# A transformer block on one Trainium2 core: attention units of eight heads with one key tile per step, and part of the transposes moved to DMA

## The chip, the cores and the metric

The kernel runs on one core of one Trainium2 chip. A core has engines that run their own instruction streams and wait for each other through semaphores: PE (TensorE, matrix multiplies; PEld is its loading of weights), ACT (ScalarE, functions of one argument such as exp), DVE (VectorE), POOL (GpSimd) and SP (SyncE, which here only issues DMA transfers). A transfer can be issued from SP's queue or from ACT's. On-chip data lies in SBUF; matmuls write to PSUM, which has eight banks of 128 x 512 f32. The metric is the device time of the whole kernel in microseconds (us). Before the change it is 1144.2, the median of 3 runs (1143.97 to 1144.4).

## The reference

One transformer block with adaptive LayerNorm, in bf16. x has 2048 tokens of D = 1024 features, there are 32 heads of 32, all of which share one key head and one value head, and the feed-forward width is F = 3584.

```python
mod = (silu(c) @ w_mod).reshape(1, 6, 1, 1024)
sa, ca, ga, sb, cb, gb = [mod[:, i] for i in range(6)]
h = layernorm(x) * (1 + ca) + sa
q = (h @ wq).reshape(B, S, 32, 32).transpose(0, 2, 1, 3)
k, v = h @ wk, h @ wv                       # one head each
p = softmax(einsum('bhqd,bkd->bhqk', q, k) * 32 ** -0.5)
a = einsum('bhqk,bkd->bhqd', p, v).transpose(0, 2, 1, 3).reshape(B, S, 1024) @ wo
x = x + ga * a
h = layernorm(x) * (1 + cb) + sb
x = x + gb * ((silu(h @ w1) * (h @ w3)) @ w2)
```

(Abridged: reshapes and types are left out.) The exponentials alone are 32 x 2048 x 2048, and they can only be computed on ACT.

## The kernel before, in words

**Tiling.** Tokens go through in eight blocks of 256 queries (`NB`, `B`). The 1024 features of q are eight groups of 128 partitions (`NC`), each of which holds four heads. There are 16 key tiles of 128 (`NTT`). A *unit* is one query block and one group of four heads, and it has eight *steps* (`NJ`), each of two key tiles. A step (`s_exp`, L822) issues eight score matmuls with 32 rows of contraction, two for each head, 256 columns wide, into two pairs of PSUM banks, and then two exponentials of 128 x 1024 on ACT into a slot of `U`, of which there are `NU` = 10. In all there are 512 steps and 1024 exponentials. The scores use six banks (`S6`, L536) as a ring of three pairs; everything else shares two banks (`PB`, L537).

**After a unit's steps** `av` (L853) multiplies the exponentials with V: 64 matmuls of 256 columns that accumulate in one bank and cannot start before the eighth step's exponentials have begun. DVE sums the exponentials over keys: `pairs` (L842) adds the two key tiles of two steps at a time (2048 elements a row), and a tree whose depth `level` (L850) gives adds the results (1024 elements); matmuls with `ONES` finish the sum over partitions. The norm is a transpose of the denominators, a copy of the values, a reciprocal, a transpose back and a multiplication, all on DVE at 256 columns. The result replaces q in `QT`.

**The start.** Loads are issued in the order of L588 to L599, nearly all from SP's queue: x tiles 0 to 3, the first half of w_mod's scale columns (`wm_dma(1, 0)`), x tiles 4 and 5, the second half, x 6 and 7, two features of wq, x 8 to 11, the two halves of the shift columns (`wm_dma(0, h)`), the other six features of wq, x 12 to 15. Only c, wk and wv come from ACT's queue. `lnt1` (L628) takes statistics of a tile of 128 tokens (DVE, POOL), normalizes it, transposes it by eight PE matmuls with `IDENT` and copies it out of PSUM, on ACT or DVE, into `HT`. `mod_cols` (L661) computes scale and shift, and copies the shift to `SAB`; `scale0` (L677) multiplies wk, wv and two features of wq by the scale; `k_bias` (L691) turns the shift into biases of q and k. `k_proj`, `v_proj` and `q_proj` (L729, L744, L759) make keys, values and queries. DMA loads split features as `(p c)`: partition p holds features 8p to 8p+7, and PE reads the normalized tile with a stride of eight elements to match.

**After a block's attention** `wo` (L916) projects, adds the residual, takes LayerNorm 2, transposes with PE into PSUM and applies scale and shift on DVE. The feed-forward part follows as *slabs* of 256 columns of w1 and w3 (L961: 32 matmuls, a tanh on ACT, two DVE operations) and *quarters* of w2 (L998, L1037: 56 matmuls of 256 columns for each quarter of the output). It is done while the next blocks' attention runs: these matmuls are the filler between score groups. The tail, after the last block's exponentials, has the last block's wo, slabs and quarters. For it w2 is loaded in two halves (`w7_dma`, L991) into the then free `U` and `W2S`.

**What sets the order.** The main program (from L1114) only describes operations and what they read and write (`Graph.op`, L55). A greedy planner (`Placer`, L185) goes through the modelled time, picks for each engine the operation with the smallest due time among those that could start soon (`choose`, L275), gives it a PSUM bank (`commit`, L307) and emits it with the waits that it needs (`emit`, L362). A table, `PLAN` (L115), has a row for every 16 steps: how long PE and the others may be kept waiting for a more urgent operation, how long values and filler may not alternate, and offsets on the due times of kinds of operation. So a change of an operation's price, size or place changes the order of everything around it, on each engine and on SP. In the trace all instructions carry line 22, the helper that plays them, and are told apart by their tiles.

Of the kernel before, what the change touches and what calls it, by code (L numbers as in the profile page):

```python
# [42 lines left out]
class Graph:  # L43
# [63 lines left out]
    def alias(self, new, old):  # L107
# [8 lines left out]
    (0.0, 0.11, 0.2, 0, 2.3, {"ln/dve": 20, "ln/act": 104, "mod/pe": -60}),  # L116
    (0.0, 0.13, 0.2, 0, 0.1,
     {"q/pe": -6, "mc/pe": 16, "pair/dve": 3, "av/dve": -10, "an/dve": -17, "slab/dve": -44, "slab/act": 35,
      "wo/dve": -9, "ln/pe": -56, "ln/dve": -21, "k/dve": 4, "mod/pe": -23}),
    (0.0, 0.15, 0.2, 1, 3.5, {"an/dve": 18}),  # L120
    (0.0, 0.15, 0.05, 1, 3.8,
     {"q/pe": -14, "mc/pe": 7, "av/dve": 44, "an/dve": -17, "slab/dve": -44, "slab/act": 35, "wo/dve": -9,
      "ln/dve": -21, "k/pe": -62, "k/dve": 4, "mod/pe": -23}),
    (0.0, 0.15, 0.2, 0, 1.1, {"wo/pe": 4, "q/pe": 1, "mc/pe": 21, "av/dve": 2, "quarter/dve": 23, "mc/dve": -3}),
    (0.0, 0.12, 0.2, 0, 1.4, {"wo/pe": 4, "q/pe": 1, "mc/pe": 21, "av/dve": 2, "quarter/dve": 23, "mc/dve": -3}),
    (0.0, 0.13, 0.2, 0, 1.2, {"av/dve": 34, "ln/dve": 20, "ln/act": 104, "mod/pe": -60, "mc/dve": 42}),
    (0.0, 0.13, 0.2, 0, 1.2, {"wo/pe": 36, "av/dve": 34, "ln/dve": 20, "ln/act": 104, "mod/pe": -60, "mc/dve": 42}),
    (0.0, 0.12, 0.2, 0, 0.8, {"wo/pe": 2, "av/dve": 34, "ln/dve": 20, "ln/act": 104, "mod/pe": -60, "mc/dve": 42}),
    (0.0, 0.12, 0.2, 0, 1.6,
     {"wo/pe": -33, "q/pe": -7, "pair/dve": 6, "wo/dve": -20, "q/dve": -43, "ln/pe": -40, "ln/dve": -10,  # L130
      "ln/act": 32, "mod/pe": -50}),
    (0.0, 0.11, 0.05, 1, 2.3,
     {"wo/pe": 4, "q/pe": 123, "pair/dve": 2, "av/dve": -22, "an/dve": 26, "slab/dve": -91, "mc/dve": -3}),
    (0.0, 0.11, 0.05, 1, 2.3,
     {"wo/pe": 4, "q/pe": 123, "pair/dve": 2, "av/dve": -22, "an/dve": 26, "slab/dve": -91, "mc/dve": -3}),
    (0.0, 0.11, 0.2, 0, 3.4, {"quarter/pe": 8, "pair/dve": 26, "slab/act": -67, "quarter/dve": -45, "mc/dve": 31}),
    (0.0, 0.11, 0.2, 0, 1.6, {"wo/pe": -55, "slab/pe": 31, "mc/pe": -5, "pair/dve": 21, "slab/dve": 16}),
    (0.0, 0.11, 0.0, 0, 2.8,
     {"quarter/pe": 8, "pair/dve": 26, "av/dve": 5, "slab/dve": -62, "slab/act": -67, "quarter/dve": -45,
      "mc/dve": 31}),  # L140
    (0.0, 0.11, 0.02, 1, 2.2,
     {"av/dve": -3, "quarter/dve": 61, "wo/dve": -13, "q/dve": -13, "ln/dve": 20, "ln/act": 104, "mod/pe": -60,
      "mc/dve": 42}),
    (0.0, 0.11, 0.02, 0, 2.6,
     {"wo/pe": -55, "slab/pe": 31, "mc/pe": -5, "pair/dve": 21, "av/dve": 20, "an/dve": 100, "slab/dve": 16,
      "quarter/dve": 84}),
    (0.0, 0.11, 0.02, 0, 2.6,
     {"wo/pe": -55, "slab/pe": 31, "mc/pe": -5, "pair/dve": 21, "av/dve": 20, "an/dve": 100, "slab/dve": 16,
      "quarter/dve": 84}),
    (0.0, 0.11, 0.02, 0, 2.6,  # L150
     {"wo/pe": -55, "slab/pe": 31, "mc/pe": -5, "pair/dve": 21, "av/dve": 20, "an/dve": 100, "slab/dve": 16,
      "quarter/dve": 84}),
    (0.0, 0.11, 0.1, 0, 2.8, {}),
    (0.0, 0.11, 0.2, 0, 1.7, {"slab/pe": 26, "mc/pe": 39, "pair/dve": -5, "slab/dve": 9, "slab/act": -76}),
    (0.0, 0.11, 0.1, 0, 1.5,
     {"wo/pe": -55, "q/pe": -15, "mc/pe": -5, "pair/dve": 21, "av/dve": 6, "slab/act": 13, "quarter/dve": -30}),
    (0.0, 0.11, 0.1, 1, 1.5,
     {"wo/pe": -55, "q/pe": -15, "mc/pe": -5, "pair/dve": 21, "av/dve": 6, "an/dve": -1, "slab/act": 13,
      "quarter/dve": -30}),
    (0.0, 0.11, 0.1, 1, 1.5,  # L160
     {"wo/pe": -55, "q/pe": -15, "mc/pe": -5, "pair/dve": 21, "av/dve": 6, "an/dve": -1, "slab/act": 13,
      "quarter/dve": -30}),
    (0.0, 0.11, 0.1, 0, 1.6, {"wo/pe": -55, "slab/pe": 31, "mc/pe": -5, "slab/act": 13, "quarter/dve": 84}),
    (0.0, 0.11, 0.05, 0, 1.8,
     {"slab/pe": -67, "quarter/pe": -25, "q/pe": -22, "pair/dve": 26, "av/dve": -15, "an/dve": -52,
      "slab/act": -67, "quarter/dve": -169, "mc/dve": 31}),
    (0.0, 0.11, 0.05, 1, 2.4, {}),
    (0.0, 0.11, 0.05, 1, 2.4, {}),
    (0.0, 0.11, 0.2, 0, 1.0,
     {"wo/pe": -55, "q/pe": -20, "mc/pe": 70, "pair/dve": 19, "slab/act": 13, "quarter/dve": -51}),  # L170
    (0.0, 0.11, 0.2, 0, 1.7,
     {"wo/pe": -28, "quarter/pe": 37, "q/pe": -20, "mc/pe": 70, "pair/dve": 19, "an/dve": -19, "slab/act": 13,
      "quarter/dve": -51}),
    (0.0, 0.11, 0.02, 0, 3.6,
     {"wo/pe": -28, "quarter/pe": 37, "q/pe": -20, "mc/pe": 70, "pair/dve": 19, "an/dve": -30, "slab/act": 13,
      "quarter/dve": -51}),
    (0.0, 0.11, 0.05, 0, 4.2,
     {"av/pe": -127, "wo/pe": -27, "quarter/pe": 39, "pair/dve": -46, "av/dve": -102, "wo/dve": 96, "q/dve": 7}),
    (0.0, 0.11, 0.2, 0, 3.2,
     {"av/pe": -127, "wo/pe": -55, "quarter/pe": 39, "q/pe": 66, "pair/dve": -46, "an/dve": 15, "wo/dve": 11,  # L180
      "q/dve": 7}),
# [3 lines left out]
class Placer:  # L185
# [121 lines left out]
    def commit(self, n, e, k, start):  # L307
# [11 lines left out]
        if e == "sp" or n.dma is not None:  # L319
            self.t[e] = start + dur  # L320
            self.bw = max(self.bw, start + 2.6) + n.nbytes / n.bw
            n.fin = self.bw + 0.5
# [119 lines left out]
def build(nc, x_in, wq_in, wk_in, wv_in, wo_in, w1_in, w3_in, w2_in, c_in, wmod_in, out, S, D, F):  # L442
# [34 lines left out]
    RB = sb("RB", [P, 2, B], F32)  # L477
# [9 lines left out]
    RC = sb("RC", [P, 8], F32)  # L487
# [8 lines left out]
    Uf = U[:].rearrange("p a b c d -> p (a b c d)")  # L496
    HTf = HT[:].rearrange("p a b -> p (a b)")
# [16 lines left out]
    GP = HTf[:, o:o + 1024].rearrange("p (s x) -> p s x", s=2)  # L514
# [10 lines left out]
           W2f[:, 0:NC * 512].rearrange("p (c f) -> p c f", c=NC)]  # L525
# [40 lines left out]

    dma("act", SCC[:, 0, :], c_in.rearrange("o (p c) -> p (o c)", p=P), "C", 2048, writes=["C0"], vt=-2000)
    for i, w in enumerate((wk_in, wv_in)):
        dma("act", WKV[:, i], pc(w), ("WKV", i), 65536, writes=[("WKV", i)], vt=-1999)

    def x_dma(tt0, cnt, vt):
# [5 lines left out]
        dma("sp", dst, x2[tt0 * P:(tt0 + cnt) * P, :].rearrange("(t p) d -> p t d", p=P), ("XL", tt0),  # L577
            cnt * P * D * 2, writes=keys, vt=vt, bw=FAST)

    def wm_dma(fld, h, vt):  # L580
        dma("sp", WM0[:, 4 * h:4 * h + 4, fld * D:(fld + 1) * D], pc(wmod_in)[:, 4 * h:4 * h + 4, fld * D:(fld + 1) * D],
            ("WM0", fld, h), 1 << 20, writes=[("WM0", fld, h)], vt=vt, bw=FAST)
# [15 lines left out]
    wq_dma(2, NC, "WQ1", -1890)  # L598
    x_dma(12, 4, -1889)  # L599
# [28 lines left out]
    def lnt1(tt, vt):  # L628
# [13 lines left out]
        static = tt < 6  # L642
# [3 lines left out]
        def tr(b=tt):  # L646
            return [lambda e, cc=cc: e.transpose(
                BANKH[b][:, cc * P:(cc + 1) * P], XN[slot].rearrange("p (q c) -> p c q", c=NC)[:, cc, :],
# [12 lines left out]
    def mod_cols(fld):  # L661
        G.tag = "mod"
        s = Sess()
        for h in range(2):
            op("pe", lambda b, h=h: [lambda e, c=c, k=k: e.matmul(
                BANK[b][:, 64 * k:64 * k + 64], WM0[:, c, fld * D:(fld + 1) * D].rearrange("p (q k) -> p k q", k=NC)[:, k, :],
                SCC[:, 3, c:c + 1].broadcast_to([P, 64]), start=(c == 0 and k == 0), stop=(c == NC - 1), skip_group_check=True)
                for c in range(4 * h, 4 * h + 4) for k in range(NC)], 0.92, reads=["C3", ("WM0", fld, h)],
# [112 lines left out]
    def mod_chunk(i, vt):  # L781
# [4 lines left out]
        if i == 1:  # L786
            G.alias([("WMB", 1)], [("XS", tt) for tt in range(6, 10)])
# [31 lines left out]
    CYC = [(n, f, j) for n in range(NB) for f in range(NC) for j in range(NJ)]  # L819
    exps = {}  # L820

    def s_exp(c):  # L822
        G.tag = "s"
        n, f, j = CYC[c]
# [3 lines left out]
        def mm():  # L828
            return [lambda e, g=g, kk=kk: e.matmul(
                BANK[2 * r[g // 2] + g % 2][:, kk * B:(kk + 1) * B],  # L830
# [350 lines left out]
```

## Time and profile before

| what | us |
|---|---|
| median of 3 runs | 1144.2 |
| profiled execution | 1143.93 |
| its span | 1142.1 |
| start of the first exponential | 32.6 |
| first scores to last scores | 32.1 to 1043.4 |
| end of the exponentials, start of the tail | 1046.1 |
| ACT busy / PE busy / DVE busy | 1024.2 / 1119.6 / 955.0 |
| the 1024 exponentials on ACT, busy | 964.8 |
| sums of exponentials on DVE, busy (2048 / 1024 wide) | 309.9 / 249.6 |

The granted clock of TensorE is 1.000. A busy time of PE is the modelled duration of pipelined matmuls that overlap, so start-to-start times are the better prices: 16 matmuls of 256 columns begin at 1065.11 and the next group at 1066.86. In groups of instructions the name before the arrow is the tile written, the names behind it are those read: `U<-S` is an exponential, `S<-QT,KT` a score, `PB<-U,V` values, `PB<-W2S,HT` a matmul of w2, `PB<-QT,W` one of a slab. W in a name stands for the weights of w1 and w3 and, in the start, of wq.

### The profile page before, as it was taken

To read this page: it belongs to the slowest core of one execution; us is meant where nothing else is said; L and a number is where in the kernel's file an instruction comes from. 1 tells how busy PE (TensorE), PEld (TensorE's weight loads), DVE (VectorE), ACT (ScalarE), POOL (GpSimd) and SP (SyncE) were. 2 spreads that over 40 slices of the span, in tenths; PEclk is the share of its full clock that TensorE was granted. 3 is DMA by queue.
4 is the path that set the end of the run, shared out by engine and by line. 5 is a ranking of instruction groups with operands and counts; after the bars stand their busy time and mean duration, and the time that the engine had idled before them with its cause. 6 is when DMAs were issued, how large, how long until landed. Compare 5 with 4: busy or idle time off the path is not lost.

```text
span 1142.1 us, 34856 instructions
## 1 busy us (share of the span) xinstructions
PE 1119.6 (98%) x15630; PEld 763.8 (67%) x15664; DVE 955.0 (84%) x1555; ACT 1024.2 (90%) x1163; POOL 36.6 (3%) x83
## 2 busy tenths in 40 slices
PE   8999999999999999999999999999999999999999
PEld 7754446666577656776677657766677666776887
DVE  7899899988988889889878989888888987888442
ACT  6999999999999999999899999999999998996110
POOL 4100000000000000000000000000000000000000
PEclk9999999999999999999999999999999999999999
DMA  9511178666396558765596468765596549667793
GB/s 343 180 52 62 38 220 215 177 186 164 81 271 191 148 130 213 225 195 144 142 264 194 142 160 227 199 194 149 133 255 189 152 116 255 200 187 202 223 291 115
DMA packets 361620, 206.32 MB, mean 181 GB/s; under 512 B 4864, under 2 KB 353280, under 8 KB 361472
## 3 DMA queue, kind: packets, MB, share of 16 engines
q1 hardware_dynamic: 361040, 203.97, 63.3%
q8 instruction: 123, 2.02, 0.7%
q14 instruction: 25, 0.20, 0.1%
q10 hardware_dynamic: 432, 0.13, 0.0%
HBM read 199.89 MB, written 4.19 MB: 179 GB/s over the span
## 4 chain that ended last, share of the span: by engine, by line
ACT 55%; PE 41%; DVE 3%; issue 0%; POOL 0%; POOLq 0%
ACT U L22 50%; PE PB L22 29%; PE S L22 12%; ACT HT L22 4%; DVE PS L22 2%; DVE QT L22 0%; DVE ST L22 0%; DVE RB L22 0%; DVE HT L22 0%; DVE X L22 0%; ACT KT L22 0%; ACT PS L22 0%; ACT XNB L22 0%; DVE XNB L22 0%; DVE RC L22 0%
## 5 line engine op out<-in xcount | busy, mean ns | idle before, releaser
L22 ACT ACTIVATE U<-S 128x1024 bf16<-128x1024 f32 x1024 | 964.8, 1117 | 17.1 <-PE PB L22 14.2
L22 DVE TENSOR_TENSOR PS<-U 128x2048 bf16<-128x2048 bf16 x256 | 309.9, 1214 | 15.6 <-ACT U L22 14.3
L22 DVE TENSOR_TENSOR PS<-PS 128x1024 bf16<-128x1024 bf16 x368 | 249.6, 686 | 4.2
L22 PE MATMUL PB<-QT,W 128*128 128x256 bf16 x1856 | 229.4, 273 | 0.2
L22 PE MATMUL S<-QT,KT 32*128 32x256 bf16 x4096 | 203.3, 273 | 5.4 <-ACT U L22 2.5
L22 PEld LDWEIGHTS PB<-QT,W 128*128 128x128 bf16 x1856 | 170.0, 98 | 47.7 <-issue 28.7
L22 PE MATMUL PB<-W2S,HT 128*128 128x256 bf16 x1512 | 191.4, 273 | 0.1
L22 PEld LDWEIGHTS PB<-W2S,HT 128*128 128x128 bf16 x1512 | 136.7, 98 | 45.2 <-issue 27.7
L22 PEld LDWEIGHTS S<-QT,KT 32*128 32x128 bf16 x4096 | 60.7, 92 | 131.9 <-ACT U L22 118.8
L22 PE MATMUL PB<-U,V 128*32 128x256 bf16 x4032 | 124.7, 273 | 1.3 <-DVE X L22 0.5
L22 PE MATMUL PB<-QT,HT 128*128 128x256 bf16 x960 | 120.0, 273 | 0.3 <-DVE HT L22 0.3
L22 PEld LDWEIGHTS PB<-U,V 128*32 128x32 bf16 x4032 | 100.0, 97 | 21.0 <-issue 7.0
L22 ACT ACTIVATE HT<-PB 128x512 bf16<-128x512 f32 (+1 forms) x110 | 78.6, 715 | 32.2 <-PE PB L22 32.2
L22 PEld LDWEIGHTS PB<-QT,HT 128*128 128x128 bf16 x960 | 88.1, 98 | 24.4 <-issue 14.3
L22 PE MATMUL PB<-HT,W 128*128 128x256 bf16 (+1 forms) x561 | 98.5, 316 | 3.5 <-issue 1.8
L22 DVE SCALAR_TENSOR_TENSOR HT<-HT,PB 128x512 bf16<-128x512 bf16 x102 | 69.3, 679 | 30.7 <-ACT HT L22 30.4
L22 DVE TENSOR_TENSOR HT<-HT,PB 128x512 bf16<-128x512 bf16 x102 | 69.6, 682 | 17.9 <-PE PB L22 17.2
L22 PEld LDWEIGHTS PB<-HT,W 128*128 128x128 bf16 x576 | 50.0, 97 | 38.3 <-issue 15.1
L22 PE MATMUL PB<-WO,QT 128*128 128x512 bf16 x213 | 54.0, 380 | 2.4 <-issue 1.3
L22 DVE STREAM_TRANSPOSE RB<-PB 128x256 f32<-128x256 f32 x63 | 28.2, 448 | 30.8 <-PE PB L22 30.8
L22 POOL TENSOR_SCALAR RS<-MV 128x1 f32<-128x1 f32 x32 | 11.5, 358 | 1018.6 <-DVE MV L22 1017.8
L22 ACT ACTIVATE HT<-S 128x512 bf16<-128x512 f32 (+1 forms) x15 | 11.0, 738 | 33.3 <-PE S L22 33.2
(112 smaller groups left out, 682.3 us busy)
## 6 DMA issues: line engine op xcount, KB each, us to landing
W<-in_B_w_dram SPq DMA_DIRECT2D x150, 512.0 KB, 4.6
W2S<-in_B_w_dram SPq DMA_DIRECT2D x28, 1792.0 KB, 8.4
HT<-in_B_w_dram SPq DMA_DIRECT2D x74, 512.0 KB, 4.6
W2S<-in_w_mod_dram SPq DMA_DIRECT2D x8, 1024.0 KB, 5.3
X<-in_A_x_dram SPq DMA_DIRECT2D x8, 512.0 KB, 6.9
U<-in_w_mod_dram SPq DMA_DIRECT2D x4, 1024.0 KB, 11.3
out_dram<-X SPq DMA_DIRECT2D x7, 512.0 KB, 8.0
U<-in_B_w_dram SPq DMA_DIRECT2D x1, 3584.0 KB, 14.0
```

The source lines that it names most:

```text
L22: return getattr(e, call[0])(*call[1], **call[2])
```

## The change

- A unit is two feature groups (eight heads). A step is one key tile: four score matmuls of 512 columns (256 queries of two feature groups). It still has two exponentials of 128 x 1024. A unit has 16 steps, and the total stays 512.
- The values come in halves of eight key tiles: 32 matmuls of 512 columns each. The first half is copied to an f32 buffer, the second is added to it. The sums over keys are adds of 2048 elements throughout; the norm is done once for two feature groups, at 512 columns.
- LN1's tiles 8 to 15 are transposed by eight DMA transposes from SP's queue instead of PE and an eviction. LN2 of blocks 1 to 6 is transposed by two DMA transposes for each block, and scale and shift are then applied in place from SBUF.
- Features are in natural order, `(c p)`, for wq, wk and wv; PE's transposes and the shift and scale columns are read without a stride. Rows of wk and wv become pieces of 64 bytes.
- The scale and shift columns of w_mod are loaded in parts of six and two chunks instead of four and four. Six features of wq and x tiles 12 to 15 are issued from ACT's queue, after c has landed. Four instead of six of LN1's tiles have a fixed bank. `PLAN` has new values.

```diff
-    def wq_dma(f0, f1, key, vt):
-        dma("sp", WQ[:, :, f0 * P:f1 * P], pc(wq_in)[:, :, f0 * P:f1 * P], key, (f1 - f0) << 18, writes=[key], vt=vt,
-            bw=FAST)
+    WSPL = (0, 6, NC)
...
+    def wq_dma(f0, f1, key, vt, eng="sp", after=()):
+        dma(eng, WQ[:, :, f0 * P:f1 * P], cp(wq_in)[:, :, f0 * P:f1 * P], key, (f1 - f0) << 18, writes=[key], vt=vt,
+            bw=FAST, after=after)
+    AL = list(G.last["C0"])
...
-    wq_dma(2, NC, "WQ1", -1890)
-    x_dma(12, 4, -1889)
+    wq_dma(2, NC, "WQ1", -1890, "act", AL)
+    x_dma(12, 4, -1889, "act", AL)
...
+        if tt >= 8:
+            o = op("sp", lambda: [lambda e: e.dma_start_transpose(HT[:, :, tt * P:(tt + 1) * P], XN[slot])], 0.5,
+                   reads=[("XN", slot)], writes=[("HT", cc, tt) for cc in range(NC)], vt=vt, dma=("HTL", slot), nbytes=1 << 18)
+            o.bw = -262144.0 / 1.0 * 1.0
+            return
-        static = tt < 6
+        static = tt < 4
...
-                for c in range(4 * h, 4 * h + 4) for k in range(NC)], 0.92, reads=["C3", ("WM0", fld, h)],
+                for c in range(WSPL[h], WSPL[h + 1]) for k in range(NC)], 0.23 * (WSPL[h + 1] - WSPL[h]), reads=["C3", ("WM0", fld, h)],
...
-    CYC = [(n, f, j) for n in range(NB) for f in range(NC) for j in range(NJ)]
+    CYC = [(n, f, k) for n in range(NB) for f in range(0, NC, 2) for k in range(NTT)]
...
-                BANK[2 * r[g // 2] + g % 2][:, kk * B:(kk + 1) * B],
-                KT[32 * g:32 * (g + 1), (2 * j + kk) * P:(2 * j + kk + 1) * P], QT[32 * g:32 * (g + 1), n, f, :],
-                start=True, stop=True, tile_position=(32 * g, 0)) for kk in range(2) for g in range(4)]
+                BANK[2 * r[g // 2] + g % 2], KT[32 * g:32 * (g + 1), k * P:(k + 1) * P],
+                QT[32 * g:32 * (g + 1), n, f:f + 2, :].rearrange("p c q -> p (c q)"),
+                start=True, stop=True, tile_position=(32 * g, 0)) for g in range(4)]
...
+    def sums(g):
+        w, c0 = g // 2, g * NJ
+        if level(w) == 2:
...
+        d = g % 3
+        for q in range(0, NJ, 2):
+            upair(3 if q else d, c0 + q)
+            if q:
+                fold(d, 3, c0 + q)
...
+                return [lambda e, h=h: e.matmul(
+                    BANK[b][32 * h:32 * (h + 1), :], V[:, NJ * hf + q, :],
+                    U[:, (g * NJ + q) % NU, h].rearrange("p c q -> p (c q)"),
+                    start=(q == 0), stop=(q == NJ - 1), tile_position=(0, 32 * h),
+                    skip_group_check=True) for h in range(4)]
...
+        if hf == 0:
+            G.tag = "an"
+            op("dve", lambda b: [lambda e: e.tensor_copy(A, BANK[b])], 0.575, reads=[("av", g)], writes=ak, vt=vt, sess=s)
+            return
...
+        op("dve", lambda b: [lambda e: e.tensor_tensor(A, A, BANK[b], ALU.add)], 0.605, reads=[("av", g)] + ak,
+           writes=ak, vt=vt, sess=s)
...
+        if 0 < n < NB - 1:
+            for t in range(2):
+                o = op("sp", lambda t=t: [lambda e: e.dma_start_transpose(h2t(n)[:, :, t * P:(t + 1) * P], XN[t])], 1.2,
+                       reads=[("XN", t)], writes=[("h2r", n, t)] + h2k(n), vt=vt - 100, waw=(t == 0), dma=("HT2", t),
+                       nbytes=1 << 18)
+                o.bw = 200e3
```

More of the change, by code (lines that the diff above doesn't have):

```diff
@@ L129 @@
[L129 to L146, printed above, removed]
@@ L182 @@
+    (0.0, 0.11, 0.2, 0, 4.5,
+     {"wo/pe": -51, "slab/pe": -9, "quarter/pe": 34, "mc/pe": -96, "pair/dve": -47, "av/dve": -16, "an/dve": 4,
+      "wo/dve": -52, "q/dve": 88}),
 ]
@@ L786, in mod_chunk @@
         if i == 1:
-            G.alias([("WMB", 1)], [("XS", tt) for tt in range(6, 10)])
+            G.alias([("WMB", 1)], [("XS", tt) for tt in range(7, 11)])
         dma("sp", WMB[r], pc(wmod_in)[:, :, c0:c0 + 512], ("WMB", r), 1 << 20,
@@ new lines, in uk, with add, upair, fold @@
+    def uk(c):
+        return [("U", c % NU, i) for i in range(2)]
+    def add(dst, a, b, ka, kb, vt, tag):
+        G.tag = tag
+        op("dve", lambda: [lambda e: e.tensor_tensor(PSW[:, dst], a, b, ALU.add)], 1.12, reads=ka + kb,
+           writes=psk(dst), vt=vt, post=0.08)
+    def upair(dst, c):
+        add(dst, UW[:, c % NU], UW[:, (c + 1) % NU], uk(c), uk(c + 1), c + 101.0, "pair")
+    def fold(dst, src, c):
+        add(dst, PSW[:, dst], PSW[:, src], psk(dst), psk(src), c + 102.0, "av")
@@ L867, in av, with avp @@
+    hold = {}
+    def avp(n):
+        if n == 0:
+            return W2f[:, 0:D].bitcast(F32), ["AVP"]
+        return GP.bitcast(F32), [("GP", 0)]
+    def av(g):
+        n, f, hf = g // NC, g % NC // 2 * 2, g % 2
+        w = g // 2
+        s = Sess(False)
+        sl = sums(g)
+        hold[g] = sl
+        G.tag = "av"
         for q in range(NJ):
             def mm(b, q=q):
-                return [lambda e, h=h, kk=kk: e.matmul(
-                    BANK[b][32 * h:32 * (h + 1), 0:B], V[:, 2 * q + kk, :], U[:, (u * NJ + q) % NU, h, kk, :],
-                    start=(q == 0 and kk == 0), stop=(q == NJ - 1 and kk == 1), tile_position=(0, 32 * h),
-                    skip_group_check=True) for kk in range(2) for h in range(4)]
@@ L873, in av @@
-            op("pe", mm, 0.2184, reads=[("V", q // 2), ("U", (u * NJ + q) % NU, 0), ("U", (u * NJ + q) % NU, 1)],
-               writes=[("av", u)], vt=-500 + u, mode="A", sess=s, post=0.145, after=[exps[(u * NJ + LAG, 1)]])
-        sd = Sess(lev > 0)
-        for q in range(NJ) if lev == 0 else ():
-            def mu(b, q=q):
-                return [lambda e, h=h, kk=kk: e.matmul(
-                    BANK[b][32 * h:32 * (h + 1), 0:B], ONES[:, 0:32], U[:, (u * NJ + q) % NU, h, kk, :],
-                    start=(q == 0 and kk == 0), stop=(q == NJ - 1 and kk == 1), tile_position=(0, 32 * h),
-                    skip_group_check=True) for kk in range(2) for h in range(4)]
-            op("pe", mu, 0.2184, reads=["ONES", ("U", (u * NJ + q) % NU, 0), ("U", (u * NJ + q) % NU, 1)],
-               writes=[("dn", u)], vt=-500 + u, mode="A", sess=sd, post=0.175, after=[exps[(u * NJ + LAG, 1)]])
@@ L884, in av @@
-        slots = list(range(0, NP, 1 << (lev - 1))) if lev else []
-        for i0 in range(0, len(slots), 2):
-            def md(b, ks=slots[i0:i0 + 2]):
-                return [lambda e, h=h, k=k: e.matmul(
-                    BANK[b][32 * h:32 * (h + 1), 0:B], ONES[:, 0:32], PS[:, k, h, :], start=(k == 0),
-                    stop=(k == slots[-1]), tile_position=(0, 32 * h), skip_group_check=True)
-                    for k in ks for h in range(4)]
-            op("pe", md, 0.109 * len(slots[i0:i0 + 2]), reads=["ONES"] + [("PS", k) for k in slots[i0:i0 + 2]],
-               writes=[("dn", u)], vt=-500 + u, mode="A", sess=sd, post=0.175)
@@ new lines, in av, with md @@
+        for x in ks:
+            def md(b, x=x):
+                return [lambda e, h=h: e.matmul(
+                    BANK[b][32 * h:32 * (h + 1), :], ONES[:, 0:32], PSW[:, x, h * 512:(h + 1) * 512], start=(x == ks[0]),
+                    stop=(x == ks[-1]), tile_position=(0, 32 * h), skip_group_check=True) for h in range(4)]
+            op("pe", md, 0.216, reads=["ONES"] + psk(x), writes=[("dn", w)], vt=-500 + g, mode="A", sess=sd, post=0.175)
+        G.tag = "an"
+        op("dve", lambda b: [lambda e: e.tensor_tensor(A, A, BANK[b], ALU.add)], 0.605, reads=[("av", g)] + ak,
+           writes=ak, vt=vt, sess=s)
```

235 lines of the change are left out of this document (133 added, 102 removed).

## The prediction

> **What bounds the kernel now.** I read the page's totals first, then the stretches around the exponentials, then the chain of waits inside the attention, then the start. Totals and the three groups that the change touches most:
>
> ```profile
> PE 1119.6 (98%) x15630; PEld 763.8 (67%) x15664; DVE 955.0 (84%) x1555; ACT 1024.2 (90%) x1163; POOL 36.6 (3%) x83
> ...
> ACT 55%; PE 41%; DVE 3%; issue 0%; POOL 0%; POOLq 0%
> ...
> L22 ACT ACTIVATE U<-S 128x1024 bf16<-128x1024 f32 x1024 | 964.8, 1117 | 17.1 <-PE PB L22 14.2
> L22 DVE TENSOR_TENSOR PS<-U 128x2048 bf16<-128x2048 bf16 x256 | 309.9, 1214 | 15.6 <-ACT U L22 14.3
> L22 DVE TENSOR_TENSOR PS<-PS 128x1024 bf16<-128x1024 bf16 x368 | 249.6, 686 | 4.2
> ```
>
> PE's 98% is a modelled share and decides nothing alone. The chain gives ACT 55% and PE 41%: the two alternate. The stretches (us, then PE, weight loads, DVE, ACT, POOL, clock, DMA share, GB/s):
>
> ```profile
> 0.00:32.50 32.50, 27.03 (x321) 23.11 (x322) 22.99 (x56) 19.28 (x20) 15.75 (x43) 1.00 0.97 337
> ...
> 540.00:560.00 20.00, 19.74 (x236) 11.76 (x238) 16.91 (x28) 15.08 (x18) 1.58 (x4) 1.00 0.46 123
> ...
> 1046.10:1142.10 96.00, 93.14 (x882) 80.01 (x880) 39.67 (x70) 8.39 (x15) 1.58 (x4) 1.00 0.79 222
> ```
>
> So there are three stages: a start of 32.6 us, in which DMA is busy 97% and no exponential runs; 1013.5 us of exponentials; a tail of 96.0 us, in which PE alone works. The middle is nearly full on both engines. The chain around its longest stop, and the sum of such stops among the waits:
>
> ```profile
> 549.05 2.92 PE PB L22 x18
> 551.97 0.05 issue
> 552.02 2.27 PE PB L22 x21
> 554.29 0.02 issue
> ```
>
> ```profile
> ACT U L22 <- PE PB L22: 14.2, 5, 4.9
> ```
>
> At 549 PE runs 39 matmul groups with no scores between them, ACT runs dry and waits up to 4.9 us. It happens five times (near 554, 681, 809, 904 and 955).
>
> **The middle, priced.** Start-to-start times from the timeline: an exponential .904 us (63 in 57.8, four short waits included); a tanh .49; a copy of a transposed tile on ACT 1.02; a matmul of 256 columns .109 (16 in 1.75, at 1065.11), of 512 columns .216 (24 in 5.18, at 1052.49); 64 value matmuls 1.76 (at 1047.13). A step's eight score matmuls take .33, and some .10 goes where PE changes kind. Between the first scores (32.1) and the last (1043.4), 1011.3 us, the instruction list of before sums to 975 on PE and 976 on ACT. The other 35 us are the five long stops (about 16 with a sixth of .9), some 40 of .27 where a unit's value matmuls stand in front of its scores, and a few at the beginning.
>
> The changed kernel's own list, in its new order, at the same prices:
> - Score steps stay 512 and exponentials 1024 of the same shape: ACT gains nothing there. Four score matmuls of 512 columns cost about what eight of 256 did, four value matmuls of 512 likewise. With the transposes taken off, PE's sum is 957 (-18). That is no gain of 18, as ACT's sum binds as well.
> - Five LN1 evictions fewer on ACT between the first and last scores: each .93 between exponentials, so -4.3 (971.7). Their cover would be a PE that is late at the same place; then the gain goes to nothing.
> - The long stops come from stretches in which PE's listed work exceeds ACT's. They are 5.2, 2.4, 3.0, 1.5, 4.4 us before (16.5; the trace shows 5.1, 2.3, 2.9, 1.6, 4.0) and 2.8, 3.5, 2.8, 2.8, 5.9 after (17.8). So the new order does not remove them. Small excesses come out 1 to 3 less. I take -2, with -6 and +3 as bounds.
> - DVE: sums 7 adds of 2048 per eight steps instead of 4 of 2048 and 6 of 1024, 560 to 534 us in all; norms 123 to 118; LN2's eight multiply-adds at .30 from SBUF against .40 from PSUM. All of it lies beside PE and ACT (DVE 84%): taken at nothing. If DVE were the limit it would be a gain of some 30.
> - LN2's DMA transposes of blocks 1 to 6 have at least twelve steps (22 us) of FFN2 matmuls between wo and the slab that reads them. They replace work on PE and are hidden, unless one takes over 15 us.
>
> **The start.** Here the trace argues against the change. The last load before the first exponential is the second part of the shift columns of w_mod: 7.5 MB stand on SP's queue up to and with it, before and after. In before it landed near 25 and what followed was:
>
> ```profile
> 27.42 2.07 PE L22 MATMUL PB<-SCC,U 128*128 128x64 bf16 x32
> ...
> 29.53 0.17 DVE L22 CAST SAB<-PB 128x8 bf16<-128x8 f32 x1 [0.47 <-PE PB L22]
> ...
> 32.59 1.93 ACT L22 ACTIVATE U<-S 128x1024 bf16<-128x1024 f32 x2
> ```
>
> Six features of wq and x tiles 12 to 15 (2.5 MB) stood behind it. The change issues them from ACT's queue as soon as c is there. Whether they then take bandwidth can be read where wk came from ACT's queue in before, 3.5 to 4.4 us:
>
> ```profile
> DMA packets 299, 0.35 MB, mean 389 GB/s; under 512 B 32, under 2 KB 160, under 8 KB 299
> ...
> q1 hardware_dynamic: 155, 0.28, 82.2%
> q10 hardware_dynamic: 144, 0.07, 25.0%
> ```
>
> 155 packets of SP against 144 of ACT: one to one, at a total that is already full (381 GB/s from 20 to 30). A rule speaks to the same point: the Trainium skill, page "DMA: Bandwidth & Descriptors", section "Issuing engines are not separate DMA queues", says that transfers started by several engines end on the same 16 DMA engines and only the issuing time is saved; by that rule too the shift columns come later by the whole 2.5 MB.
>
> Sum: 2.62 million bytes at 381 GB/s are 6.9 us. wk and wv in pieces of 64 bytes instead of 512 are 128 packets for each DMA engine; at about 8 ns (c's packets of 16 bytes) 1.0, less .45 before. Landing 25 + 7.5 = 32.5. Behind it are 16 matmuls instead of 32 (the load is now split 6 + 2), and the copy to SAB at about 34.5 instead of 29.5. From SAB to the first exponential before took 3.06; two features are now projected for the first step, 16 matmuls more, 1.75. First exponential at 39.3: **+6.5** (bounds: -2 if the loads do not compete and SP's 5.5 us of issuing at 5.55 are saved; +9 if statistics of tiles 8 to 11, which stand before SAB on DVE, end late too, or ACT is held by its two large issues).
>
> **LN1's DMA transposes.** Eight on SP, behind WO and the w_mod chunks on that queue (4 MB, 11 us at 381). The last four tiles are normalized about 38 to 42, so tile 12 lands about 52 to 54. Its keys are projected on PE just ahead of step 7, due about 51. PE executes in order, so scores behind it wait. I take **+1** (0 to +5). No transpose by DMA is in the trace; the nearest row is the x load of 512 KB, 6.9 us from issue to landing. Several in flight together land closer than that, and I take this end.
>
> **The tail.** After the last scores 144 instead of 110 FFN2 matmuls of block 6 are left: 34 x .109 = 3.7; with pairs normalized at 512, **+3.9** (0 to +7). It is all on PE, with nothing beside it. The second half of the last w2 starts 19.2 us before its use instead of 22.7; a landing takes 16.0, so this adds nothing until it is 3 late.
>
> **Sum.** The profiled execution took 1143.9 (span 1142.1 and 1.8 around it; the median of three is 1144.2): 1143.9 + 6.5 + 1 - 4.3 - 2 + 3.9 = **1149.0**.
>
> **The rivals.**
> - *The loads do not compete (faster).* If ACT's queue gets only gaps, or the first exponential depends on something earlier, it comes within 1 us of 32.6. Then 1143.9 + 0 - 4.3 - 2 + 1.5 = 1139. For it: SP's issuing really stands still for 5.46 at 5.55. Against: 97% DMA share and the one-to-one row. It decides from a first exponential before about 35.
> - *Slow transposes.* If eight in series each cost 6.9, they run 55 us from about 36 to 91, while the last key tile is needed at step 15, about 66: +25, or 1165 to 1175 with the rest. Against: 512 KB loads overlap on the queue. In the Trainium skill, "VectorE: DVE Perf Modes", section "The three transpose paths" gives 1309 ns for a 128x128 block by DMA: an estimate of 84 us for eight tiles of eight blocks in series, and of about 1200 for the kernel; "Advanced Engine Details and Errata", section "X-Bar Transpose (TRN2)", calls them as fast as other DMAs; no run yet shows it.
> - *Half of it (no change).* If half of the 2.5 MB lands after the shift columns, the first exponential is 3 late: 1145.5.
>
> **How the numbers follow.** About 0.2%, 2.3 us, is what a measurement can tell from no change. Forecast .52 (1146 to 1156, with its upper part for a later start and early stalls); loads not competing .25; slow transposes .13; half .10. Faster: nearly all of the second, .24; same: the fourth and the forecast's lower edge, .16; slower .60. The range 1137 to 1160 leaves out the slow transposes and a few per cent on either side; the forecast's own is 1146 to 1156.
>
> **What would show it.** First exponential near 39 and SAB near 34.5, with ACT's queue taking half of the packets from 5 to 20; five stops of ACT of 2.5 to 6 us; 144 matmuls of W2S after the last scores and a tail near 100; landings of the transposes before their projections, and no wait of PE near step 7 beyond 5 us. A first exponential near 33, a PE that stands for tens of us at the key projections, or a middle that shrinks towards PE's 957 would prove it wrong.

## The result, and the profile after

The changed kernel takes 1162.7 us (median of 4 runs, 1161.3 to 1163.6) against 1144.1 before: 1.0162 times as long (95% interval 1.0150 to 1.0174), or 18.6 us more. The forecast was 1149.0 in a range of 1137 to 1160. The sign was right, the size was not, and the range missed the time by 2.7.

Totals and groups on the page of the changed kernel:

```profile
span 1160.9 us, 25561 instructions
...
PE 1114.8 (96%) x11091; PEld 685.7 (59%) x11120; DVE 947.5 (82%) x1240; ACT 1018.9 (88%) x1158; POOL 49.1 (4%) x83
...
ACT 64%; PE 25%; DVE 6%; DMA 4%; issue 1%; SPq 0%; POOL 0%; DVEq 0%
...
L22 ACT ACTIVATE U<-S 128x1024 bf16<-128x1024 f32 x1024 | 963.2, 1132 | 20.6 <-PE S L22 12.3
```

PE, DVE and ACT have less work than before (4.8, 7.5 and 5.3 us less; POOL has 12.5 more), and the whole is 18.8 us longer. DMA, which was not in the chain that ended last, now has 4% of it, and DVE has 6% instead of 3%. The stretches of the changed kernel (us, then PE, weight loads, DVE, ACT, POOL, clock, DMA share, GB/s):

```profile
0.00:41.40 41.40, 29.06 (x325) 22.66 (x326) 23.43 (x58) 17.95 (x19) 16.13 (x43) 0.88 0.92 279
41.40:100.00 58.60, 48.34 (x559) 23.64 (x563) 45.43 (x73) 50.29 (x58) 3.46 (x8) 0.88 0.43 112
100.00:1060.70 960.70, 940.17 (x9327) 556.84 (x9350) 837.14 (x1039) 942.32 (x1070) 27.93 (x28) 1.00 0.65 177
1060.70:1160.90 100.20, 97.19 (x884) 82.56 (x883) 41.45 (x71) 8.36 (x14) 1.58 (x4) 1.00 0.78 224
```

The start is 8.9 longer, the tail 4.3, and in the first 59 us of exponentials ACT is busy for only 50. Taken apart, with a wait counted as the time from one ACT instruction's start to the next beyond the first one's price (.904 for an exponential, .478 for a tanh, .37 for a key eviction, .93 for a tile's eviction; waits over .08):

| us | before | after | difference | forecast |
|---|---|---|---|---|
| first exponential | 32.6 | 41.5 | +8.9 | +6.5 |
| ACT's waits before 100 us | 2.1 | 9.1 | +7.0 | +1 |
| ACT's work between first and last exponential | 977.0 | 972.7 | -4.3 | -4.3 |
| ACT's waits after 100 us | 30.7 | 32.7 | +2.0 | -2 |
| what is left of the middle (spacing) | | | +1.0 | 0 |
| tail behind the last exponential | 96.0 | 100.3 | +4.3 | +3.9 |

The start, in the timeline of the changed kernel:

```profile
34.99 2.18 PE L22 MATMUL PB<-SCC,U 128*128 128x64 bf16 x64 [0.29 <-ACT HT L22]
...
37.21 0.17 DVE L22 CAST SAB<-PB 128x8 bf16<-128x8 f32 x1 [1.32 <-PE PB L22]
...
41.46 1.02 ACT L22 ACTIVATE U<-S 128x1024 bf16<-128x1024 f32 x1
```

and DMA from 8 to 20 us:

```profile
DMA packets 3196, 4.47 MB, mean 372 GB/s; under 512 B 562, under 2 KB 1873, under 8 KB 3195
...
q1 hardware_dynamic: 1599, 2.70, 63.3%
q10 hardware_dynamic: 1596, 1.75, 43.2%
...
U<-in_w_mod_dram SPq DMA_DIRECT2D x1, 512.0 KB, 16.3
```

SP's queue (q1) and ACT's (q10) moved 1599 and 1596 packets, one to one, at a total of 372 GB/s (371 from 10 to 20 us before). The last row is the second part of the shift columns: issued at 17.5, it landed 16.3 later, at 33.8 instead of 25.7.

The chain of waits behind the first exponentials:

```profile
46.71 0.53 DVE XNB L22
47.24 0.03 DVE MV L22
47.27 11.25 DMA HT<-XNB
...
58.62 0.55 DVE XNB L22
59.16 0.21 DVE V L22
...
59.42 0.39 PE PB L22 x8
59.81 0.55 PE S L22 x4
```

Read from below: the scores at 59.8 follow eight matmuls of V, which wait for a PSUM bank that DVE's eviction of V frees. That eviction stands on DVE behind the normalization of tile 15, which writes the buffer that tile 12's DMA transpose still reads. The transpose was issued at 47.27 and took 11.25 us. ACT waits 7.2 us there (counted as in the table; the row has 7.03 of idle time), and 1.2 at the next scores.

```profile
60.41 1.94 ACT L22 ACTIVATE U<-S 128x1024 bf16<-128x1024 f32 x2 [7.03 <-PE S L22]
```

The stretches around it (columns as above) show what DMA did meanwhile:

```profile
41.00:50.00 9.00, 6.86 (x111) 4.72 (x111) 6.73 (x18) 8.91 (x12) 2.34 (x6) 1.00 0.99 310
50.00:55.00 5.00, 2.01 (x65) 1.60 (x61) 1.17 (x3) 3.37 (x4) 1.13 (x3) 0.65 1.21 349
55.00:60.00 5.00, 0.58 (x12) 0.40 (x12) 1.39 (x5) 0.00 (x0) 0.00 (x0) 0.50 1.16 147
```

### The profile page after: what moved, and what is told of

Its sections match the earlier page's. It is cut to its first block, busy times and chain, and to the rows that moved or that the text cites. A ratio compares the mean times of both kernels' runs of the same rounds, so it can differ in the third digit from the quotient of the medians.

```text
span 1160.9 us, 25561 instructions
## 1 busy us (share of the span) xinstructions
PE 1114.8 (96%) x11091; PEld 685.7 (59%) x11120; DVE 947.5 (82%) x1240; ACT 1018.9 (88%) x1158; POOL 49.1 (4%) x83
## 4 chain that ended last, share of the span: by engine, by line
ACT 64%; PE 25%; DVE 6%; DMA 4%; issue 1%; SPq 0%; POOL 0%; DVEq 0%
ACT U L22 60%; PE PB L22 16%; PE S L22 10%; ACT HT L22 4%; DVE PS L22 3%; DMA W<-in_A_wq_dram 2%; DMA HT<-XNB 1%; DVE HT L22 1%; DMA W2S<-in_B_w_dram 1%; DVE QT L22 1%; DVE ST L22 0%; SPq L22 0%; DVE X L22 0%; DVE RB L22 0%; ACT XNB L22 0%
## 5 line engine op out<-in xcount | busy, mean ns | idle before, releaser
L22 DVE TENSOR_TENSOR PS<-PS 128x2048 bf16<-128x2048 bf16 x180 | 219.5, 1219 | 2.5
L22 PE MATMUL S<-QT,KT 32*128 32x512 bf16 x2048 | 202.6, 386 | 13.2 <-ACT U L22 10.3
L22 PE MATMUL PB<-W2S,HT 128*128 128x256 bf16 x1456 | 182.5, 274 | 0.0
L22 PEld LDWEIGHTS PB<-W2S,HT 128*128 128x128 bf16 x1456 | 132.0, 98 | 46.4 <-issue 31.6
L22 PEld LDWEIGHTS S<-QT,KT 32*128 32x128 bf16 x2048 | 51.4, 91 | 161.1 <-ACT U L22 153.0
L22 PE MATMUL PB<-U,V 128*32 128x512 bf16 x2048 | 130.0, 381 | 1.5 <-DVE QT L22 0.7
L22 DVE TENSOR_TENSOR HT<-HT,PB 128x512 bf16<-128x512 bf16 (+1 forms) x129 | 88.0, 683 | 17.4 <-PE PB L22 14.4
L22 PEld LDWEIGHTS PB<-U,V 128*32 128x32 bf16 x2048 | 46.5, 96 | 61.0 <-issue 18.7
L22 POOL TENSOR_SCALAR RS<-MV 128x1 f32<-128x1 f32 x32 | 18.1, 565 | 1018.2 <-DVE MV L22 1018.0
L22 DVE BATCH_NORM_STATS2 ST<-X 128x6 f32<-128x512 bf16 x44 | 28.3, 681 | 8.8 <-DMA X<-in_A_x_dram 8.3
```

Source lines behind the costliest of these rows:

```text
L22: return getattr(e, call[0])(*call[1], **call[2])
```

## The experiments

How they were made: in all but the two that put LayerNorm back on PE, PE, DVE, POOL and ACT compute in the order of the kernel that the run starts from, to the last instruction. This is what *same order* means: the planner runs as it does, and then only entries of SP's list of transfers (or of ACT's) are moved, or matmuls left out of the tail. In the run with the loads on SP the edit stands ahead of the planner, which gives the same order of computing all the same. The code shown is cut: "..." stands for lines left out. The table has all of the runs. The time is the median of four (or a single run, in brackets); first exponential, waits before 100 us and tail (all in us) are those of one profiled execution. That was the fastest of the four with loads on SP (1156.4), in the queue by need (1153.2) and with x 12 between (1147.7), so there these columns and the time do not belong together to better than 1 to 3 us.

| run | first exp. | waits before 100 | tail | time |
|---|---|---|---|---|
| before | 32.6 | 2.1 | 96.0 | 1144.1 |
| changed | 41.5 | 9.1 | 100.3 | 1162.7 |
| before, loads on ACT | 40.2 | 1.7 | 96.0 | 1151.5 |
| loads on SP | 36.5 | 8.8 | 100.6 | 1158.6 |
| transposes first | 42.0 | 6.8 | 100.3 | 1159.6 |
| loads on SP, transposes first | 36.6 | 9.5 | 100.3 | 1156.5 |
| loads on SP, wo last | 36.5 | 2.7 | 100.3 | 1151.8 |
| queue by need | 34.1 | 8.1 | 100.3 | 1154.5 |
| x 12 between | 35.1 | 1.0 | 100.3 | 1150.5 |
| LN1 on PE | 34.9 | 1.2 | 100.3 | (1156.2) |
| LN2 on PE | 40.1 | 8.7 | 116.9 | (1190.0) |
| 34 fewer in the tail | 36.9 | 3.5 | 100.1 | 1150.2 |
| 17 fewer, late | 34.4 | 5.6 | 98.6 | (1150.1) |

**The late start: two loads, one edit in each direction.** The first run takes them off ACT's queue in the changed kernel:

```diff
-    wq_dma(2, NC, "WQ1", -1890, "act", AL)
-    x_dma(12, 4, -1889, "act", AL)
+    wq_dma(2, NC, "WQ1", -1890)
+    x_dma(12, 4, -1889)
```

> The changed kernel with wq's other six features and x tiles 12 to 15 back on SP's queue, behind the shift columns; every engine's order else as it was. Theory A (ACT's queue takes half of the DMA engines from SP's): the two features of wq land near 19 instead of 25.8, the shift columns near 27 instead of 33.8, first exponential 34.5 to 36 instead of 41.5, whole kernel 5.5 to 7 us faster than the changed one, about 1156. Rival B (the start is late because of its own work: three times the projections before the first scores, a PE at a lowered clock, small pieces of wk and wv): first exponential stays at 39 or later, kernel 1160 or more.

The two features of wq landed at 18.7 and the shift columns at 26.8, 7.0 earlier. The first exponential came at 36.5, 5.0 earlier, and the kernel took 1158.6 (1156.4 to 1159.8). Rival B falls, but 2 us of the landing's gain did not arrive. The timeline shows where they went: the first DMA transpose now stood behind these two loads on SP and landed at 34.5, and DVE waited for its buffer ahead of the eviction of q.

```profile
35.05 0.55 DVE L22 TENSOR_SCALAR PS<-W2S,MV,RS 128x1024 bf16<-128x1024 bf16 x1 [4.28 <-DMA HT<-PS]
...
36.49 1.02 ACT L22 ACTIVATE U<-S 128x1024 bf16<-128x1024 f32 x1 [3.31 <-PE S L22]
```

The second run (same order) puts the two loads onto ACT's queue in the kernel before:

```diff
...
+    spq = pl.ops["sp"]
+    moved = [f for f in spq if f.n.dma in ("WQ1", ("XL", 12))]
+    pl.ops["sp"] = [f for f in spq if f not in moved]
+    at = next(i for i, f in enumerate(pl.ops["act"]) if f.n.wk == ("C1",)) + 1
+    pl.ops["act"][at:at] = moved
```

> The kernel before with only these two loads issued from ACT's queue after the first tanh, all orders of computing kept. Theory A: 2.5 MB at 381 GB/s, so the shift columns land near 32.5 instead of 25.7, first exponential 38 to 39.5 instead of 32.6, kernel about 1150 (+5.5 to +7). Rival B: landing within 1.5 us of before and the kernel within 1145.5.

Shift columns at 32.6 (25.7 before, so 6.9 later: what 2.62 million bytes take at 381 GB/s), first exponential at 40.2, middle and tail as before to .1 us, kernel 1151.5: 1.0065 times before (1.0048 to 1.0082). The first exponential in the timeline of this kernel:

```profile
40.22 1.02 ACT L22 ACTIVATE U<-S 128x1024 bf16<-128x1024 f32 x1
```

These two lines of the change, put alone into the kernel before, cost 7.4 us. This is shown, not argued. From 10 to 20 us ACT's queue moved 1180 packets there and SP's 1175, one to one again. The Trainium skill, "DMA: Bandwidth & Descriptors", section "Issuing engines are not separate DMA queues", says that transfers of several engines interleave on the same 16 DMA engines; the 6.9 us, and the 1599 packets against 1596 in the changed kernel, agree.

**The early stop: what stands ahead of the transposes.** Same order; the four loads of 1 MB behind LN1's fourth transpose go behind the eighth:

```diff
...
+    late = [f for f in spq if f.n.dma[0] == "WMB"][:2] + [f for f in spq if f.n.dma[0] == "WO"]
+    rest = [f for f in spq if f not in late]
+    at = max(i for i, f in enumerate(rest) if f.n.dma[0] == "HTL") + 1
+    pl.ops["sp"] = rest[:at] + late + rest[at:]
```

> The changed kernel with the four loads of 1 MB (wo and the first two chunks of w_mod) moved on SP's queue from between LN1's fourth and fifth DMA transpose to behind the eighth; all orders of computing kept. Theory C (the early stop is tile 12's transpose waiting behind these 4 MB): tile 12's transpose lands 4 to 5 us after its issue, near 52 instead of 58.5, the waits before 100 us fall from 9.1 to about 2.5, the kernel is 6 to 7 us faster than the changed one, about 1156. Rival D (a DMA transpose is slow in itself, or holds DVE whatever is ahead of it): the waits stay above 6 and the kernel at 1160 or more.

The first half of the theory held better than expected: tile 12's transpose landed 3.0 after its issue, at 50.8, and DVE did not wait. But the waits fell only to 6.8, and the time to 1159.6, which by the expectation is nearer to rival D than to theory C. A row of this kernel's timeline says why:

```profile
60.60 1.89 PE L22 MATMUL PB<-SCC,W2S 128*128 128x64 bf16 x32 [5.06 <-DMA W2S<-in_w_mod_dram]
```

The first w_mod chunk that I had moved is wanted by PE right there, ahead of the scores, and it landed at 60.6. A wait took the place of the wait. With the loads on SP as well:

> The changed kernel with both edits: loads on SP and transposes ahead of the four loads. Theories A and C add up: first exponential 34.5 to 36, waits before 100 us about 2.5, kernel 1149 to 1151, still slower than before by the tail (+4.2) and the waits of the middle. If x tiles 12 to 15, which land near 34 in this order, are late for their statistics, 2 to 3 more.

First exponential 36.6, the same wait for the chunk (4.5 us on PE), 1156.5. The expectation of 1149 to 1151 failed, through the same step.

So the two parts of what I had moved had to be told apart. Loads on SP, same order, and only wo's two loads go behind the eighth transpose:

```diff
...
+    late = [f for f in spq if f.n.dma[0] == "WO"]
...
```

> The changed kernel with the loads of wq and x tiles 12 to 15 on SP, and wo's two loads moved behind the eighth transpose, while the first two chunks of w_mod stay ahead of the fifth. Theory C (bytes ahead on the queue): 2 MB less ahead of tile 12's transpose, which lands near 48.5 instead of 53.5, and the w_mod chunk still lands near 44, ahead of its use; waits before 100 us fall from 8.8 to about 4, kernel about 1153.5. Rival D (transposes hold DVE by themselves): waits stay near 8.8, kernel 1157 or more.

Tile 12's transpose landed at 47.5 and the chunk at 43.7. The waits before 100 us fell from 8.8 to 2.7, the time from 1158.6 to 1151.8 (1151.0 to 1153.4). Theory C holds, rival D falls: nothing about the transposes was changed except for 2 MB ahead of them. (Between the two profiled executions, 1156.4 and 1152.3, the gain is only 4.1, as the waits after 100 us are 3.3 longer in this one.) The chain that lasted 11.25 in the changed kernel, in this one:

```profile
42.33 0.03 DVE MV L22
42.36 5.12 DMA HT<-XNB
...
47.57 0.55 DVE XNB L22
48.12 0.21 DVE V L22
```

Then I tried to put everything in the order in which it seemed to be needed: four transposes, wq and x 12 to 15, one w_mod chunk, four transposes, the rest.

```diff
...
+    pl.ops["sp"] = rest[:at] + tr[:4] + big + wmb[:1] + tr[4:] + wmb[1:2] + wos + rest[at:]
```

> As the run before, and also the loads of wq and x 12 to 15 moved from ahead of LN1's first four transposes to behind them, and only one w_mod chunk ahead of the fifth; computing in the same order. If the order on the queue is the whole cause of the late start and of the early stop: tile 8's transpose lands about 4 us after its issue instead of 8, DVE is not held ahead of the q evictions, first exponential 33 to 34.5 (36.5 with the loads ahead), waits before 100 us 2 to 3, kernel 1147 to 1150. If the start is bound by its own work at a lowered clock: first exponential 36 or later, kernel 1153 or more.

The first exponential came at 34.1, as expected: most of the late start is a matter of the queues, not of the start's own work. Of the 8.9 us, 5.0 went with the two loads and 2.4 with the order on SP's queue; 1.5 are left. But the waits were 8.1 and the time 1154.5. Rows of this kernel's timeline:

```profile
40.77 2.72 PE L22 MATMUL PB<-SAB,W 128*128 128x64 bf16 x48 [4.59 <-DMA W<-in_A_wq_dram]
43.38 1.88 DVE L22 BATCH_NORM_STATS2 ST<-W2S 128x6 f32<-128x512 bf16 x3 [7.00 <-DMA W2S<-in_A_x_dram]
```

wq's other features are wanted by the matmuls of the bias, which PE has ahead of the third step. Moved behind four transposes, whose issue has to wait for DVE, the load came at 40.6. The mended order leaves wq where it was and puts only x 12 to 15 between the second and the third transpose:

```diff
...
+    pl.ops["sp"] = rest[:at] + tr[:2] + x12 + tr[2:4] + wmb[:1] + tr[4:] + wmb[1:2] + wos + rest[at:]
```

> As the run with wo's loads last, with x tiles 12 to 15 moved from ahead of LN1's first transposes to between the second and the third, and one w_mod chunk instead of two ahead of the fifth. wq's load stays ahead, as its bias is wanted by PE near 40. The first transpose should land near 33 instead of 34.6, so DVE is held less ahead of the q evictions: first exponential 34.5 to 35.5 instead of 36.5, waits before 100 us 2.5 to 4, kernel 1150 to 1151. If tiles 12 to 15 then come late for DVE: waits 5 or more and 1152 or more.

First exponential 35.1, waits before 100 us 1.0, kernel 1150.5 (1147.7 to 1150.6):

```profile
35.06 1.02 ACT L22 ACTIVATE U<-S 128x1024 bf16<-128x1024 f32 x1 [1.03 <-PE S L22]
...
40.70 11.09 ACT L22 ACTIVATE U<-S 128x1024 bf16<-128x1024 f32 x12
```

The profile is of the execution of 1147.7; the other three took 1150.4 to 1150.6, and the last run below, whose early order is the same, shows 5.6 us of waits before 100 us. So the 1.0 holds for the fastest execution alone. By the median this is the fastest complete form of the changed kernel that I found, 12.2 us faster than the changed kernel by the queue and the order of 14 transfers alone. It is still 1.0049 times the kernel before (1.0034 to 1.0064): no version beats it.

**What the DMA transposes are worth.** Loads on SP, LN1's tiles 8 to 15 back on PE, ordered anew by the planner with the same table:

```diff
...
-        if tt >= 8:
+        if False:
             o = op("sp", lambda: [lambda e: e.dma_start_transpose(HT[:, :, tt * P:(tt + 1) * P], XN[slot])], 0.5,
...
```

> The changed kernel with the loads on SP and tiles 8 to 15 of LN1 transposed on PE with an eviction on ACT or DVE, as before; the planner orders it anew. By the theory no wait on a transpose: first exponential 34 to 35.5, waits before 100 us 2 to 4. By the instruction lists the middle is 9.6 dearer (2.8 of work on ACT, 6.8 of stretches in which PE has more to do), so the whole comes to 1156 to 1160: what the DMA transposes save and what they cost in waits are about the same. Rival: the early waits stay, 1163 or more.

Much as expected: first exponential 34.9, waits 1.2, ACT's work 2.8 more and later waits 6.5 more than with the loads on SP, 1156.2. With the loads on SP and the queue else as the change has it, the transposes are about even (1156.4 to 1159.8 with them, a single run of 1156.2 without); with the queue mended they gain 5.7 (1150.5). Part of that may be the table, which was made for the kernel with transposes.

LN2 of blocks 1 to 6 back on PE, else the changed kernel:

```diff
...
-        if 0 < n < NB - 1:
+        if False:
...
```

> The changed kernel with LN2 of blocks 1 to 6 transposed on PE as before; the planner orders it anew and leaves 336 instead of 256 matmuls of W2S behind the last scores. If the tail is priced by what is left to PE: tail 100.3 + 8.7 + 3 = 112, the middle 10 dearer by the lists, kernel about 1184. If the tail's growth is something else (a late load of w2, the wide norm): tail below 105. If LN2's transposes by DMA had cost time in the middle, the middle would get shorter.

1190.0: the middle 12.1 longer, the tail 16.6. The tail has 106 matmuls more (11.6 at .109) and a wait of 3.6 for the second half of the last w2:

```profile
PE S L22 <- DMA W2S<-in_B_w_dram: 3.6, 1, 3.6
```

The twelve LN2 transposes of the changed kernel took 3.0 to 5.8 us each from issue to landing and nothing in the chain waits for them. That they save the 27 us of this difference is not shown, as the order is another one.

**The tail.** The forecast priced it by 34 more matmuls of block 6 left behind the last scores. Same order as with wo last; 34 of them, the first ones behind the last scores, are left out:

```diff
...
+    last_s = max(i for i, f in enumerate(pl.ops["pe"]) if f.n.mode == "S")
+    left = 34
+    for f in pl.ops["pe"][last_s:]:
+        if left and f.n.wk and f.n.wk[0][:2] == ("f2", NB - 2) and len(f.calls) == 2 and not f.calls[0][2]["start"]:
+            del f.calls[0]
+            left -= 1
```

> As the run with wo's loads last, but 34 of the 144 FFN2 matmuls of block 6 that stand behind the last scores are left out (two feature groups' worth of terms is missing from those sums, so that part of the output is incomplete). If the tail is priced by the matmuls left to PE: 34 x .109 = 3.7 less, tail 96.6 instead of 100.3, kernel 1148 instead of 1151.8. If it is bound by w2's load or the last norm: tail stays above 99.

The tail stayed at 100.1. In its timeline PE now waits where those matmuls had been:

```profile
1051.40 0.40 PE L22 MATMUL S<-PS,ONES 128*32 128x512 bf16 x4 [0.46 <-DVE PS L22]
1052.60 1.05 PE L22 MATMUL S<-W2S,HT 128*128 128x256 bf16 x8 [0.81 <-DMA W2S<-in_B_w_dram]
...
1055.45 5.79 PE L22 MATMUL S<-WO,QT 128*128 128x512 bf16 x26 [0.50 <-DVE QT L22]
...
1065.45 1.07 PE L22 MATMUL PB<-IDENT,XNB 128*128 128x128 bf16 x16 [1.06 <-DVE XNB L22]
```

With the matmuls in place (wo last) the only wait of PE in these rows is .20, for the load of w2. They were cover: they filled the time in which PE would have waited for the last sums, the last norm and the last LN2. So the simple price had failed for these. But the timelines of the two kernels differ further on: among the last block's slabs before has 6 matmuls of W2S, the changed kernel 36. So the other 17 that could be left out were taken from there (with x 12 between; the same filter, from the first slab on):

> As the run with x 12 to 15 between the transposes, with 17 of the 36 FFN2 matmuls of block 6 left out that stand among the last block's slabs (part of the terms of those sums is missing). If these, unlike the 34 that stood ahead of wo and LN2, cover nothing: tail 100.3 - 17 x .109 = 98.4. If they too cover waits: tail 100.0 or more.

Tail 98.6, 1.7 less, where 17 x .109 is 1.85. These cover nothing. If all 30 more matmuls among the slabs cost that price, they are +3.3 of the tail's +4.3. The other +1.0 lies ahead of the first slab (19.0 us behind the last exponential before, 20.0 with x 12 between); that the last norm on DVE makes it is argued, not shown.

## Why the prediction was wrong, step by step

- **What bounds the kernel, and the stages**: right for the start, the tail and the exponentials from 100 us on, which change by -1.3 in all (-4.3 + 2.0 + 1.0). But the stage of exponentials as a whole is 5.7 longer (1019.2 instead of 1013.5), through the 7.0 us of waits in its first 59 us.
- **The start, +6.5**: mechanism right and shown in both directions; the term was too small by 2.4, near the edge of its bounds (-2 to +9). The working has two slips of its own: the landing before was at 25.7, not near 25, and its 39.3 is 6.7 behind 32.6, not 6.5. The shift columns landed at 33.8 (32.5 forecast). SAB then took 3.4 instead of 2, because PE had all 64 matmuls of the columns behind the landing, not 16, and behind a tile's eviction on ACT. From SAB to the first exponential it took 4.2 (4.8 forecast). What the small pieces of wk and wv cost is at most what is left with the loads on SP: the columns at 26.8 instead of 25.7, 1.1 (.55 forecast).
- **LN1's DMA transposes, +1 (0 to +5)**: this step failed, and with it the range. It measured +7.0. The 4 MB ahead of tile 12 were in the working, and so was the order of what follows, but two things in it were wrong. First the time: tiles 12 to 15 were to be normalized at 38 to 42, and tile 12 to land at 52 to 54. Tile 12 was normalized at 46.7, and it landed at 58.5. SP issued the four loads only behind the fourth transpose, which follows DVE's normalization of tile 11, at 41.0 to 42.9; the last of them landed at 57.7, 16.7 us behind the first issue, where 11 at 381 GB/s were forecast. The three stretches shown above have 310, 349 and 147 GB/s; why the last of them is so slow was not tried. Second the wait: the engine that waited was not PE at tile 12's keys, but DVE at the buffer that tile 15 shares with tile 12, with V's evictions queued behind it.
- **Rival "slow transposes"**: its price of 6.9 us each in series was wrong. With nothing ahead of it a transpose of 256 KB took 3.0 us (tile 12 with the transposes first), and the first four landings with the loads on SP are .9 to 1.7 apart. The estimate from "VectorE: DVE Perf Modes" of the Trainium skill (section "The three transpose paths", 10.5 us for eight blocks) is too long for this case; "Advanced Engine Details and Errata", section "X-Bar Transpose (TRN2)", which calls them as fast as other DMAs, agrees better: a load of 512 KB took 4.8 (the median of the weight loads in the changed kernel). The rival's 1165 to 1175 lies nearer to the measured 1162.7 than the forecast does, but that is luck: transposes that are slow in themselves are not what the runs show.
- **ACT's evictions, -4.3**: right to .1.
- **The long stops**: five were forecast from the two lists, 2.8, 3.5, 2.8, 2.8 and 5.9 long. The trace has 2.4 near 502, 2.9 in pieces near 614, 2.4 near 757, 2.4 near 884 and 5.3 near 1032. The -2 for the small waits did not come; the later waits are 2.0 more in this execution, and .5, 2.5 and 3.8 more with the loads on SP, with x 12 between and with wo last. This is 4.0 of the miss, the second largest part, and its cause stays open.
- **DVE and LN2's transposes at nothing**: no transpose of LN2 stands in the chain. But DVE's share of the chain rose from 3 to 6%, most of it from 100 us on (its sums of exponentials have 3.2% of the chain between 100 and 1060 us, 1.7% before). Whether the later waits come from there was not tried.
- **The tail, +3.9**: +4.3 measured, but the working was only partly right. 34 x .109 priced matmuls of which those ahead of wo and LN2 are cover and cost nothing; the 17 tried among the slabs cost their price. That the sum of the two came out near +3.9 is in part luck.
- **Loads not competing**: refuted by the two runs that move only these loads, one in each direction.
- **The whole miss**: 13.7 us between 1149.0 and 1162.7 are 6.0 from LN1's transposes, 4.0 from the later waits, 2.4 from the start, 1.0 from spacing and .4 from the tail (13.8 by the rounded terms).

One thing stays open: executions of the changed kernel's forms differ by up to 3.4 us where those of before differ by at most 1.1. Two profiles of the same early order (x 12 between, and 17 fewer, late) have the landing of tile 11's transpose at 39.2 and at 42.0, and in the second PE waits for it:

```profile
42.05 1.05 PE L22 MATMUL PB<-HT,PS 128*128 128x256 bf16 x8 [3.59 <-DMA HT<-PS]
```

That DMA landings now stand in the chain explains that they count. What makes them differ was not tried.

## What to carry to other kernels

Moving a load to another engine's queue made it a competitor of everything that was on its way, packet for packet (1599 and 1596 here): ask what the first result waits for, and put behind it whatever is not needed for it. A small transfer that replaces work of an engine takes over the engine's place in the order only if nothing large stands ahead of it in its queue (11.25 us to land with 4 MB issued ahead of it, 5.12 with 2 MB, 3.0 with nothing); follow its issue, its landing, the buffer that it holds and what is queued behind the next writer of that buffer. And work that is left over at the end costs its price only where it covers nothing: look at which rows of the tail have waits before you multiply.

## What was not expected of the hardware

The granted clock of PE was 1.000 throughout before. In the changed kernel it was .83 from 10 to 20 us and .71 from 20 to 30 (PE busy 5.9 of 10 in both; 7.9 and 8.6 before), and .50 from 55 to 65, behind the stop of 7.4 us. PE's busy time in such a stretch does not settle its clock: with the loads on SP PE was busy 6.2 from 10 to 20 us at a clock of 1.00, and in the kernel before with the loads on ACT 6.5 at .71. Eight projections of 256 columns took 1.87 us at .50 (at 60.95), and 1.05 at 65.44, where the clock is .99. In the kernel before with the loads on ACT, the clock was .71 and .67 in the same stretches, and the first exponential came 7.6 later where the landing was 6.9 later. The late load thus cost somewhat more than its lateness; how much of that is the clock was not separated.

SP's issuing also stands still in the start: the issue of x tiles 8 to 11 took 9.6 us in the changed kernel, where ACT's queue was loaded too, and 5.5 before, and everything that SP issues later waits for it.
